# A causal convolution and a SwiGLU block on one core: the opening is put together anew

## The chip, the cores and the metric

The kernel runs on one core of one Trainium2 chip. Each core has a matrix engine (TensorE, PE in the profile, with its weight loads as PEld), a vector engine (VectorE, DVE), a scalar engine (ScalarE, ACT), a general engine (GpSimd, POOL) and a queue engine that issues transfers (SyncE, SP). Every engine works through its own instructions in the order in which the program gives them; they meet through semaphores. The metric is the time of one execution on the device in microseconds (us), the median of several runs.

## The reference

The input `x` has 8 sequences of 4096 tokens with 192 channels. Eight heads of 24 channels each have 7 taps, and the taps go through a softmax:

```python
w = np.exp(weight - np.max(weight, axis=-1, keepdims=True))
w = w / (np.sum(w, axis=-1, keepdims=True) + 1e-09)
x_pad = np.concatenate([np.zeros((B, pad, D)), x], axis=1)
out = np.einsum('hk,bskhg->bshg', w, x_unf)      # causal, 7 taps, per head
g = x @ w_gate                                   # x: the result above, 32768 x 192
silu = g * (1.0 / (1.0 + np.exp(-g)))
return silu * (x @ w_val) @ w_out                # 192 -> 1536 -> 192
```

All inputs and the output are float32. The kernel's products take fp16 operands and add up in float32.

## The kernel before

The 32768 tokens are cut into 32 pairs of 1024 tokens, each pair into two blocks of 512 (`TB`). A block goes through 12 chunks (`NCH`) of 128 hidden channels. In a chunk, `Block.first` makes gate and value products (L517 and L518) from the convolved block, `Block.gate` runs SiLU on ScalarE (L522) and the product with the value on VectorE (L524), and `Block.second` adds pieces of the output product (L529) of the block before, so that the second product of a block runs during the first product of the next. Blocks 0 and 1 together have chunks 0 to 23; "chunk 12" is the first chunk of block 1.

TensorE writes into eight banks of PSUM. In the steady part these are two banks for gates, three for values, one named `run` for the convolution's running sum, and two for the output sums. In block 0 the gates of the chunks listed in `PLAN["third"]` use the bank `run` as a third gate bank, which puts them in line with the convolution that uses it too.

The convolution of later pairs is done on the vector engines by three groups of channels and tokens: A (channels 0 to 127, first block), B (channels 128 to 191, both blocks) and C (channels 0 to 127, second block). Transfers (`emit_load`, issued at L103) bring x as 32 x 32 squares into `sqA` and `sqB`; a VectorE transpose (`emit_turn`, L114) makes `xtA` and `xtB`; then ScalarE starts a running sum and makes products (L444, L437), VectorE adds taps to it (L454, the last one writes `aD`), GpSimd makes the other products and adds everything up (L459, L466), and writes `xc` (L472). Two transfers (`swapped`, L420 and L421) make a copy `xs` with the halves of the partitions exchanged. `at_chunk` writes down behind which chunk each of these steps is issued; `PLAN["opening"]` gives these chunks for pair 1 (turn, start, ScalarE taps, VectorE taps, GpSimd taps, join, swap), and `PLAN["load"]` gives the chunks of the loads of later pairs, counted from the pair's own first chunk, chunk 8 at the earliest.

Pair 0 is made another way, on TensorE. The taps land in `taps`, go through the softmax (L232 to L240), and are repeated into `left`, in a high and a low fp16 part. The four `repeat` products (L306) spread them over token rows and `cut_band` (L314) cuts bands out of them, which gives the matrices `T`. `heads` and `halves` (products at L327) multiply windows of x by these bands. Block 0's x is cast into `x16`, block 1's into `x16p` (two casts on GpSimd, L227). For block 0 the sums go through `foldA`, `foldC` and `gather` (L370) to `D0`, `D1`, `D2`, the operands of the first 12 chunks. For block 1, `lateA(0)`, `lateA(1)` and `lateC` do this between the chunks of block 0, with two copies (`foldA1`, `foldC1`) and two exchanges by transfer (`swapA1`, `swapC1`, L632). The taps in a third form, `parts`, go through two small products (L391) and a sum (L397) to `wn`, the scalars that the vector engines' convolution uses from pair 1 on.

`warm` issues products of zeros on the bank `idle`. The program's order is the order of issue on every engine. A transfer waits in its queue for its data, and what stands behind it waits with it: `mark` (L414) puts an empty instruction into SP's queue that waits for the last piece of a first quarter of the output product, and the first piece of the next quarter on the same half of the array waits for that instruction. The first weights (chunks 0 to 3), the next (4 to 7), the last (8 to 11) and the output weights are loaded through GpSimd's queue (L162 and L569).

## Time and profile before

| | us |
|---|---|
| median of 3 runs | 778.95 (777.58 to 778.97) |
| the profiled execution | 780.57 |
| its span, first to last instruction | 778.8 |
| TensorE busy in the span | 766.3 (98%) |
| VectorE, ScalarE, GpSimd busy | 658.2, 659.0, 667.9 |
| granted TensorE clock, mean over the span | 0.996 |

The page divides the span into 40 slices of 19.5 us; a digit gives the busy tenths of a slice. A row of the list of groups reads: line, engine, operation, output and input by the program's names, shape, count, then busy time and the mean of one in ns, then the idle time ahead of it and what ended that. The chain of work follows the last instruction back to what released it, step by step. A busy TensorE isn't a TensorE at its peak: the granted clock and the distance between starts tell that.

The opening of the profiled execution has these times: first filler on TensorE 0.99, taps landed 3.41, first `repeat` product 6.39, first `heads` product 8.65, first gate product 12.15, chunk 0's second step 12.79, block 1's first product 27.43, first pieces of the output product 29.95.

### The profile page before, as it was taken

To read this page: it belongs to the slowest core of one execution; us is meant where nothing else is said; L and a number is where in the kernel's file an instruction comes from. 1 tells how busy PE (TensorE), PEld (TensorE's weight loads), DVE (VectorE), ACT (ScalarE), POOL (GpSimd) and SP (SyncE) were. 2 spreads that over 40 slices of the span, in tenths; PEclk is the share of its full clock that TensorE was granted. 3 is DMA by queue.
4 is the path that set the end of the run, shared out by engine and by line. 5 is a ranking of instruction groups with operands and counts; after the bars stand their busy time and mean duration, and the time that the engine had idled before them with its cause. 6 is when DMAs were issued, how large, how long until landed. Compare 5 with 4: busy or idle time off the path is not lost.

```text
span 778.8 us, 28276 instructions
## 1 busy us (share of the span) xinstructions
PE 766.3 (98%) x11033; PEld 531.3 (68%) x11033; DVE 658.2 (85%) x1041; ACT 659.0 (85%) x1189; POOL 667.9 (86%) x654
## 2 busy tenths in 40 slices
PE   7799999999999999999999999999999999999998
PEld 3576666666666666666766766666666666666666
DVE  5688888888888888888888888888888888888975
ACT  5688888888888888888888888888888888888875
POOL 6589988899888899888898888898888898888850
PEclk9899999999999999999999999999999999999999
DMA  9434443433443344443444443444443344343211
GB/s 151 87 78 88 84 97 83 87 89 83 87 99 82 80 94 84 89 97 81 83 87 90 87 92 83 84 84 96 84 92 88 80 85 95 83 94 87 64 46 53
DMA packets 255336, 67.27 MB, mean 86 GB/s; under 512 B 207975, under 2 KB 255201, under 8 KB 255201
## 3 DMA queue, kind: packets, MB, share of 16 engines
q1 hardware_dynamic: 252329, 63.69, 38.6%
q0 software_dynamic: 2800, 1.77, 1.7%
q8 instruction: 86, 1.41, 0.8%
q14 instruction: 49, 0.40, 0.2%
q10 hardware_dynamic: 72, 0.00, 0.0%
HBM read 29.64 MB, written 25.17 MB: 70 GB/s over the span
## 4 chain that ended last, share of the span: by engine, by line
PE 96%; DMA 1%; DVE 1%; POOL 1%; SPq 0%; issue 0%; ACT 0%; DVEq 0%; ACTq 0%
PE gate L517 57%; PE acc L529 32%; PE val L518 7%; DMA sqB<-in_x_dram 1%; DMA taps<-in_weight_dram 0%; POOL t L466 0%; SPq L103 0%; PE acc L724 0%; POOL t L459 0%; ACT L233 0%; PE val L724 0%; PE run L724 0%; PE acc L327 0%; DVE xtB L114 0%; DVE aD L454 0%
## 5 line engine op out<-in xcount | busy, mean ns | idle before, releaser
L524 DVE TENSOR_TENSOR h<-silu,val 128x512 f16<-128x512 f16 x768 | 509.4, 681 | 107.5 <-ACT silu L522 78.1
L522 ACT ACTIVATE silu<-gate 128x512 f16<-128x512 f32 x768 | 453.1, 594 | 99.4 <-PE val L518 82.7
L466 POOL TENSOR_TENSOR t<-t,t 128x512 f32<-128x512 f32 x310 | 393.4, 1269 | 59.7 <-ACT t L437 39.2
L518 PE MATMUL val<-xc,w_sb 64*128 64x512 f16 x1116 | 410.3, 377 | 0.0
L517 PE MATMUL gate<-xc,w_sb 64*128 64x512 f16 x1116 | 409.9, 376 | 0.0
L529 PEld LDWEIGHTS <-h 64*128 64x128 f16 x6048 | 292.5, 94 | 125.9 <-SPq L414 2.8
L529 PE MATMUL acc<-wo_sb,h 64*128 64x192 f16 x6048 | 364.7, 243 | 2.4 <-SPq L414 2.3
L518 PE MATMUL val<-xs,w_sb 64*128 64x512 f16 x1116 | 360.4, 377 | 0.0
L517 PE MATMUL gate<-xs,w_sb 64*128 64x512 f16 x1116 | 360.2, 376 | 0.0
L517 PEld LDWEIGHTS <-w_sb 64*128 64x128 f16 x2340 | 213.0, 94 | 104.5 <-issue 2.6
L518 PEld LDWEIGHTS <-w_sb 64*128 64x128 f16 x2340 | 210.9, 95 | 3.5 <-issue 3.3
L472 POOL TENSOR_TENSOR xc<-t,aD 128x512 f16<-128x512 f32 x93 | 118.0, 1269 | 7.3
L459 POOL TENSOR_SCALAR t<-xtA,wn 128x512 f32<-128x512 f32 x155 | 105.6, 691 | 9.2 <-DVE xtA L114 9.2
L437 ACT ACTIVATE t<-xtA,wn 128x512 f32<-128x512 f32 x124 | 88.5, 714 | 0.0
L567 ACT COPY o<-acc 128x384 f32<-128x384 f32 x126 | 60.3, 479 | 6.3 <-PE acc L529 3.4
L459 POOL TENSOR_SCALAR t<-xtB,wn 128x512 f32<-128x512 f32 x62 | 42.2, 694 | 4.5 <-DVE xtB L114 4.5
L454 DVE SCALAR_TENSOR_TENSOR aD<-xtA,wn,run 128x512 f32<-128x512 f32 x62 | 46.0, 742 | 0.0
L437 ACT ACTIVATE t<-xtB,wn 128x512 f32<-128x512 f32 x62 | 44.2, 713 | 0.0
L444 ACT ACTIVATE run<-xtA,wn 128x512 f32<-128x512 f32 x62 | 42.5, 686 | 0.0
L114 DVE STREAM_TRANSPOSE xtA<-sqA 128x544 f32<-128x544 f32 (+1 forms) x48 | 34.6, 721 | 0.0
L454 DVE SCALAR_TENSOR_TENSOR run<-xtB,wn,run 128x512 f32<-128x512 f32 x31 | 23.2, 750 | 0.2 <-ACT run L444 0.2
L454 DVE SCALAR_TENSOR_TENSOR run<-xtA,wn,run 128x512 f32<-128x512 f32 x31 | 23.2, 750 | 0.0
(105 smaller groups left out, 185.8 us busy)
## 6 DMA issues: line engine op xcount, KB each, us to landing
out_dram<-o SPq DMA_DIRECT2D x127, 192.0 KB, 2.0
sqA<-in_x_dram SPq DMA_DIRECT2D x92, 132.0 KB, 3.1
xs<-xc SPq DMA_DIRECT2D x186, 64.0 KB, 2.0
sqB<-in_x_dram SPq DMA_DIRECT2D x96, 68.0 KB, 2.3
headA<-in_x_dram SPq DMA_DIRECT2D x28, 128.0 KB, 2.6
headB<-in_x_dram SPq DMA_DIRECT2D x14, 68.0 KB, 2.2
headB<-in_x_dram SPq DMA_DIRECT2D x14, 64.0 KB, 2.0
w_sb<-in_moe_w_gate_dram POOLq DMA_DIRECT2D x3, 192.0 KB, 5.8
```

What stands on the lines that cost most here:

```text
L437: mul(parts[-1], *self.tap(k))
L444: nc.scalar.mul(self.aD, *self.tap(0))
L454: nc.vector.scalar_tensor_tensor(out=self.aD, in0=v, scalar=s, in1=run, op0=ALU.mult, op1=ALU.add)
L459: self.product(k, lambda t, v, s: nc.gpsimd.tensor_scalar(t, v, scalar1=s, scalar2=1.0, op0=ALU.mult, op1=ALU.mult), self.parts)
L466: nc.gpsimd.tensor_tensor(self.parts[0], self.parts[0], t, op=ALU.add)
L472: nc.gpsimd.tensor_tensor(xc, self.parts[0], self.aD, op=ALU.add)
L517: nc.tensor.matmul(g, w[0:DB, ca, f], a[0:DB, :], start=(i == 0), stop=(i == 2))
L518: nc.tensor.matmul(v, w[DB:P, cb, f], b[DB:P, :], start=(i == 0), stop=(i == 2))
L522: nc.scalar.activation(s, self.g.pop(j), AF.Silu)
L524: nc.vector.tensor_tensor(h, s, self.v.pop(j), op=ALU.mult)
L529: ins = nc.tensor.matmul(acc, self.h[j][r, ts(s, P)], wo_r[r, j, :], start=first and j == 0, stop=not first and j == NCH - 1, skip_group_c ...
L567: nc.scalar.copy(self.o[:, 2 * half : 2 * half + 2, :], self.acc[:, :, 0:D])
```

## The change

Taps: the transfer brings 8 rows of 7 instead of 64 rows with each head repeated eight times. A product with a mask `whose` (a new iota and two VectorE operations) writes the 64 rows into the bank `D2`; the maximum and the exponential read them there. `soft` gets an eighth column that holds 1e-9, and the sum over it is made on VectorE, in place of ScalarE's accumulation and an addition on GpSimd. The masks are made from integers by a helper `where`; the mask `band` is now made behind the maximum. A first exponential of a constant is issued behind the taps' transfer.

Order: three fillers stand ahead of the product with `whose` and three behind it, the one behind the repeats is gone, and short ones stand between the heads and a full one behind the gathers. The first weights for values are loaded right behind those for gates. ScalarE casts the first half of block 0's windows and GpSimd the second. `own` is copied on GpSimd. Block 1's x (`load_x(1, 0, NW)`) and the squares for group B are issued on SP behind the first `repeat` product; before, the x went out at the start and the squares behind the first heads. `parts` and the clearing of `x16p`'s other half are made on VectorE behind D1's copy, and the two small products for `wn` stand behind all the gathers.

Chunks: `lateA(0)` moves from 3 to 2, the second half of pair 1's A squares from behind `lateC` (8) to 9, group A's turn from 9 to 10, group B's swap from 14 to 12, the gates in the `run` bank from 2, 6, 9 to 2, 7, 10. The loads of pair 2 move from 8, 8, 14 and 20 to 10, 16, 18 and 21.

```diff
     opening=(
-        (9, 12, (13, 14), (13, 14), 12, 14, 20),
-        (2, 3, (4, 5), (3, 4), 4, 5, 14),
+        (10, 12, (13, 14), (13, 14), 12, 14, 20),
+        (2, 3, (4, 5), (3, 4), 4, 5, 12),
...
-    gate=2, val=3, lead=4, third=(2, 6, 9),
+    gate=2, val=3, lead=4, third=(2, 7, 10),
...
-    taps = const_pool.tile([RT, K], fp32, tag="taps", name="taps")
-    nc.scalar.dma_start(
-        out=taps[:, :],
-        in_=weight.unsqueeze(1).to_broadcast([H, 8, K]),
-    )
+    taps = const_pool.tile([H, K], fp32, tag="taps", name="taps")
+    nc.scalar.dma_start(out=taps, in_=weight)
...
-    load_x(1, 0, NW)
...
+    two = const_pool.tile([P, 1], fp32, tag="two", name="two")
+    nc.scalar.activation(two, one, AF.Exp)
...
+    head = numbers("head", [H, RT], [[1, RT]], 0, int32, -8)
...
+    def where(out, t, bits):
+        if bits:
+            nc.vector.tensor_scalar(t, t, scalar1=bits, scalar2=None, op0=ALU.bitwise_and)
+        nc.vector.tensor_scalar(out, t, scalar1=0.0, scalar2=None, op0=ALU.is_equal)
+
+    where(whose, head, -8)
+    where(rotate, far, 7)
+    where(pick[:, :, :].rearrange("r h m -> r (h m)"), row, 0)
...
     load_w(0, 4, 0)
+    load_w(0, 4, 1)
...
-    nc.vector.tensor_reduce(wmax, taps, axis=AX.X, op=ALU.max, negate=True)
-    nc.scalar.activation(soft, taps, AF.Exp, bias=wmax, accum_out=wsum)
-    nc.gpsimd.tensor_scalar(wsum, wsum, scalar1=1e-9, scalar2=None, op0=ALU.add)
+    warm(3)
+    rows = early["D2"][0:RT, 0:K]
+    nc.tensor.matmul(rows, whose, taps, start=True, stop=True)
+    nc.vector.tensor_reduce(wmax, rows, axis=AX.X, op=ALU.max, negate=True)
+    nc.scalar.activation(soft[:, 0:K], rows, AF.Exp, bias=wmax)
+    where(band, off, -8)
     nc.vector.memset(parity(x16p[:, 0, :, :], 1), 0.0)
...
+    nc.vector.tensor_reduce(wsum, soft, axis=AX.X, op=ALU.add)
...
-    cast(nc.gpsimd.tensor_copy, 0, 3)
-    load_w(0, 4, 1)
-    cast(nc.scalar.copy, 3, NW)
+    cast(nc.scalar.copy, 0, 3)
+    nc.scalar.activation(two, one, AF.Silu)
+    cast(nc.gpsimd.tensor_copy, 3, NW)
...
-    nc.scalar.copy(
+    nc.gpsimd.tensor_copy(
         own[:, :].rearrange("h (t c) -> h t c", t=2),
...
-    warm(6)
-    repeat(0, 0)
+    warm(3)
+    repeated_first = repeat(0, 0)
+
+    sync_after(nc.sync.nop(), repeated_first, "the rest after block 0's x")
+    load_x(1, 0, NW)
+    if n_pairs > 1:
+        for part in (2, 3):
+            emit_load(1, part, None)
     repeat(1, 0)
     repeat(0, HH)
     repeat(1, HH)
-    warm(1)
...
-    some = heads(0, 0)
-
-    if n_pairs > 1:
-        sync_after(nc.sync.nop(), some, "squares after x")
-        for part in (2, 3):
-            emit_load(1, part, None)
+    heads(0, 0)
+    warm(1, 2)
     heads(0, 1)
+    warm(1, 2)
     nc.scalar.copy(foldA, sums[0])
     heads(1, 0)
+    warm(1, 2)
     heads(1, 1)
...
+    gather("D1", 2, foldC, first=False)
+    gather("D2", 3, foldC)
+    warm(1)
+    nc.vector.tensor_copy(D1, early["D1"])
+    nc.scalar.copy(D2, early["D2"])
+    nc.vector.memset(parity(x16p[:, 1, :, :], 0), 0.0)
+
+    parts = const_pool.tile([RT, 3, K], fp16, tag="parts", name="parts")
+    raw, rest = (const_pool.tile([RT, K], fp32, tag=n, name=n) for n in ("raw", "rest"))
+    nc.vector.tensor_tensor(raw, soft[:, 0:K], norm.to_broadcast([RT, K]), op=ALU.mult)
+    nc.vector.tensor_copy(parts[:, 0, :], raw)
+    nc.vector.tensor_tensor(rest, raw, parts[:, 0, :], op=ALU.subtract)
+    nc.vector.tensor_copy(parts[:, 1, :], rest)
+    nc.vector.tensor_tensor(parts[:, 2, :], rest, parts[:, 1, :], op=ALU.subtract)
...
-    gather("D1", 2, foldC, first=False)
-    gather("D2", 3, foldC)
-    nc.vector.tensor_copy(D1, early["D1"])
-    nc.scalar.copy(D2, early["D2"])
...
-        if n_pairs > 1:
-            for part in (0, 1):
-                emit_load(1, part, 1)
...
-    at_chunk(3, lambda: lateA(0))
+    at_chunk(2, lambda: lateA(0))
     at_chunk(5, lambda: lateA(1))
     at_chunk(5, outA)
     at_chunk(8, lateC)
+    if n_pairs > 1:
+        for part in (0, 1):
+            at_chunk(9, lambda part=part: emit_load(1, part, 1))
...
-            at_chunk(max(base + c, 8), lambda q=q, part=part: emit_load(q, part))
+            c = {2: 10, 3: 16, 0: 18, 1: 21}[part] if q == 2 else base + c
+            at_chunk(c, lambda q=q, part=part: emit_load(q, part))
```

More of the change, by code (lines that the diff above doesn't have):

```diff
@@ L167, with numbers @@
     nc.vector.memset(one, 1.0)
+    two = const_pool.tile([P, 1], fp32, tag="two", name="two")
+    nc.scalar.activation(two, one, AF.Exp)
     nc.vector.memset(x_sb[0:pad, 0, 0, :], 0.0)
-    def numbers(name, shape, pattern, base, dt=fp32):
+    def numbers(name, shape, pattern, base, dt=int32, step=1):
         t = const_pool.tile(shape, dt, tag=name, name=name)
         nc.gpsimd.iota(
-            t, pattern=pattern, base=base, channel_multiplier=1, allow_small_or_imprecise_dtypes=True
+            t, pattern=pattern, base=base, channel_multiplier=step, allow_small_or_imprecise_dtypes=True
         )
         return t
-    far = numbers("far", [RT, 8, K], [[-1, 8], [1, K]], 8, int32)
+    head = numbers("head", [H, RT], [[1, RT]], 0, int32, -8)
+    far = numbers("far", [RT, 8, K], [[-1, 8], [1, K]], 8)
     row = numbers("row", [RT, RT], [[-1, RT]], 0)
-    off = numbers("off", [P, W], [[-1, W]], -(K // 2))
-    nc.vector.tensor_scalar(far, far, scalar1=7, scalar2=None, op0=ALU.bitwise_and)
+    off = numbers("off", [P, W], [[-1, W]], 0)
+    whose = const_pool.tile([H, RT], fp32, tag="whose", name="whose")
     rotate = const_pool.tile([RT, 8, K], fp32, tag="rotate", name="rotate")
-    nc.vector.tensor_scalar(rotate, far, scalar1=0.0, scalar2=None, op0=ALU.is_equal)
     pick = const_pool.tile([RT, H, 8], fp16, tag="pick", name="pick")
-    nc.vector.tensor_scalar(
-        pick[:, :, :].rearrange("r h m -> r (h m)"), row, scalar1=0.0, scalar2=None, op0=ALU.is_equal
-    )
-    nc.vector.tensor_tensor(off, off, off, op=ALU.mult)
     band = const_pool.tile([P, W], fp16, tag="band", name="band")
-    nc.vector.tensor_scalar(band, off, scalar1=float((K // 2) ** 2), scalar2=None, op0=ALU.is_le)
+    def where(out, t, bits):
[5 more added lines that the diff above has]
+    where(pick[:, :, :].rearrange("r h m -> r (h m)"), row, 0)
     plain = const_pool.tile([P, 4, grp], fp16, tag="plain", name="plain")
@@ L202 @@
     plain = plain[:, :, :].rearrange("p h c -> p (h c)")
+    nc.gpsimd.memset(spread, 0.0)
     load_w(0, 4, 0)
-    nc.gpsimd.memset(spread, 0.0)
+    load_w(0, 4, 1)
     mask = const_pool.tile([RT, D], fp16, tag="mask", name="mask")
-    nc.gpsimd.memset(mask, 0.0)
-    nc.gpsimd.affine_select(
-        out=mask[:, :].rearrange("r (h c) -> r h c", h=H),
-        in_=mask[:, :].rearrange("r (h c) -> r h c", h=H),
-        pattern=[[-8, H], [0, grp]],
-        compare_op=ALU.not_equal, fill=1.0, base=0, channel_multiplier=1,
-    )
     x16 = xpool.tile([P, NW, D + 8], fp16, tag="x16", name="x16", bufs=1)
@@ L230, with warm @@
     wmax, wsum, norm = (const_pool.tile([RT, 1], fp32, tag=n, name=n) for n in ("wmax", "wsum", "norm"))
-    soft = const_pool.tile([RT, K], fp32, tag="soft", name="soft")
-    nc.vector.tensor_reduce(wmax, taps, axis=AX.X, op=ALU.max, negate=True)
-    nc.scalar.activation(soft, taps, AF.Exp, bias=wmax, accum_out=wsum)
-    nc.gpsimd.tensor_scalar(wsum, wsum, scalar1=1e-9, scalar2=None, op0=ALU.add)
+    soft = const_pool.tile([RT, K + 1], fp32, tag="soft", name="soft")
+    nc.vector.memset(soft[:, K : K + 1], 1e-9)
+    opening = ctx.enter_context(ExitStack())
+    pool0 = opening.enter_context(tc.tile_pool(name="early", bufs=1, space=bass.MemoryType.PSUM))
+    early = {
+        n: pool0.tile([P, TB], fp32, tag=n, name=n)
+        for n in ("hiA", "loA", "hiC", "loC", "idle", "D2", "D0", "D1")
+    }
+    def warm(n, r=SUBS):
+        for _ in range(n):
+            nc.tensor.matmul(
+                early["idle"][:, 0 : r * P].rearrange("p (r c) -> p r c", c=P), zeros,
+                zeros.unsqueeze(1).to_broadcast([P, r, P]), start=True, stop=True,
+            )
+    warm(3)
[4 more added lines that the diff above has]
+    where(band, off, -8)
     nc.vector.memset(parity(x16p[:, 0, :, :], 1), 0.0)
     spun = const_pool.tile([RT, 8, K], fp32, tag="spun", name="spun")
-    nc.vector.tensor_tensor(spun, rotate, soft.unsqueeze(1).to_broadcast([RT, 8, K]), op=ALU.mult)
+    nc.vector.tensor_tensor(spun, rotate, soft[:, 0:K].unsqueeze(1).to_broadcast([RT, 8, K]), op=ALU.mult)
     turned = const_pool.tile([RT, 8], fp32, tag="turned", name="turned")
+    nc.vector.tensor_reduce(wsum, soft, axis=AX.X, op=ALU.add)
     nc.vector.tensor_reduce(turned, spun, axis=AX.X, op=ALU.add)
@@ L254 @@
     left = left[:, :, :, :].rearrange("r i n m -> r i (n m)")
-    two = const_pool.tile([P, 1], fp32, tag="two", name="two")
+    cast(nc.scalar.copy, 0, 3)
     nc.scalar.activation(two, one, AF.Silu)
-    cast(nc.gpsimd.tensor_copy, 0, 3)
-    load_w(0, 4, 1)
-    cast(nc.scalar.copy, 3, NW)
-    own = const_pool.tile([RT, P], fp16, tag="own", name="own")
-    nc.scalar.copy(
-        own[:, :].rearrange("h (t c) -> h t c", t=2),
-        mask[:, P:D].unsqueeze(1).to_broadcast([RT, 2, DB]),
-    )
-    nc.scalar.copy(
-        parity(x16p[:, 1, :, :], 0),
-        zeros[:, 0:grp].unsqueeze(1).unsqueeze(1).to_broadcast([P, NW, 4, grp]),
-    )
+    cast(nc.gpsimd.tensor_copy, 3, NW)
     for k, lo, hi, at in ((0, 0, DB, 0), (1, DB, 96, 0), (2, 0, 32, 32), (3, 32, 96, 0)):
@@ L272 @@
         )
-    parts = const_pool.tile([RT, 3, K], fp16, tag="parts", name="parts")
-    raw, rest = (const_pool.tile([RT, K], fp32, tag=n, name=n) for n in ("raw", "rest"))
-    nc.gpsimd.tensor_tensor(raw, soft, norm.to_broadcast([RT, K]), op=ALU.mult)
-    nc.gpsimd.tensor_copy(parts[:, 0, :], raw)
-    nc.gpsimd.tensor_tensor(rest, raw, parts[:, 0, :], op=ALU.subtract)
-    nc.gpsimd.tensor_copy(parts[:, 1, :], rest)
-    nc.gpsimd.tensor_tensor(parts[:, 2, :], rest, parts[:, 1, :], op=ALU.subtract)
     load_w(4, 8, 0)
     load_w(4, 8, 1)
-    opening = ctx.enter_context(ExitStack())
-    pool0 = opening.enter_context(tc.tile_pool(name="early", bufs=1, space=bass.MemoryType.PSUM))
-    early = {
-        n: pool0.tile([P, TB], fp32, tag=n, name=n)
-        for n in ("hiA", "loA", "hiC", "loC", "idle", "D2", "D0", "D1")
-    }
-    def warm(n, r=SUBS):
-        for _ in range(n):
-            nc.tensor.matmul(
-                early["idle"][:, 0 : r * P].rearrange("p (r c) -> p r c", c=P), zeros,
-                zeros.unsqueeze(1).to_broadcast([P, r, P]), start=True, stop=True,
-            )
+    nc.gpsimd.memset(mask, 0.0)
+    nc.gpsimd.affine_select(
+        out=mask[:, :].rearrange("r (h c) -> r h c", h=H),
+        in_=mask[:, :].rearrange("r (h c) -> r h c", h=H),
+        pattern=[[-8, H], [0, grp]],
+        compare_op=ALU.not_equal, fill=1.0, base=0, channel_multiplier=1,
+    )
+    own = const_pool.tile([RT, P], fp16, tag="own", name="own")
+    nc.gpsimd.tensor_copy(
+        own[:, :].rearrange("h (t c) -> h t c", t=2),
+        mask[:, P:D].unsqueeze(1).to_broadcast([RT, 2, DB]),
+    )
     T = const_pool.tile([P, 2, H, W], fp16, tag="T", name="T")
@@ L388 @@
     nc.scalar.copy(D0, early["D0"])
+    gather("D1", 2, foldC, first=False)
[11 more added lines that the diff above has]
+    nc.vector.tensor_tensor(parts[:, 2, :], rest, parts[:, 1, :], op=ALU.subtract)
+    wn = const_pool.tile([P, 2, K], fp32, tag="wn", name="wn")
     taps_ps = early["idle"][:, 0 : 6 * K].rearrange("p (g t k) -> p g t k", g=2, k=K)
@@ L391 @@
         nc.tensor.matmul(taps_ps[:, g, :, :], which, parts, start=True, stop=True)
-    gather("D1", 2, foldC, first=False)
-    gather("D2", 3, foldC)
-    nc.vector.tensor_copy(D1, early["D1"])
-    nc.scalar.copy(D2, early["D2"])
-    wn = const_pool.tile([P, 2, K], fp32, tag="wn", name="wn")
     nc.vector.tensor_reduce(wn, taps_ps.rearrange("p g t k -> p g k t"), axis=AX.X, op=ALU.add)
```

## The prediction

> **What bounds the kernel now.** I read the page first, then TensorE's waits over the first 80 us, then the clock in short stretches, then the chain of work and the transfer queue of the opening.

> ```profile
> span 778.8 us, 28276 instructions
> PE   7799999999999999999999999999999999999998
> PEclk9899999999999999999999999999999999999999
> PE 96%; DMA 1%; DVE 1%; POOL 1%; SPq 0%; issue 0%; ACT 0%; DVEq 0%; ACTq 0%
> ```

> TensorE is full from about 40 us to the end, so a microsecond won in the first two slices is a microsecond off the span, and nothing later can be won. The change touches only those slices. What TensorE waits for there (total us, times, longest):

> ```profile
> PE hiA L306 <- DVE left L249: 2.6, 1, 2.6
> PE gate L517 <- DVE aD L454: 2.5, 1, 2.5
> PE acc L529 <- SPq L414: 2.3, 1, 2.3
> PE val L518 <- DVE h L524: 0.6, 2, 0.3
> ```

> Three holes: before the first product, at gate chunk 6, and in block 1 before the third quarter of the second product. The next rows show a second price of the last two. Columns: stretch, its length, busy of PE, PEld, DVE, ACT, POOL (instructions), granted clock, DMA share, GB/s.

> ```profile
> 14.95:18.40 3.45, 3.19 (x113) 1.69 (x112) 2.38 (x5) 1.20 (x3) 0.12 (x1) 1.00 1.41 180
> 18.40:21.80 3.40, 0.93 (x28) 0.57 (x14) 2.94 (x5) 3.26 (x6) 3.24 (x4) 1.00 1.14 147
> 21.90:22.10 0.20, 0.20 (x4) 0.10 (x2) 0.00 (x0) 0.20 (x1) 0.20 (x1) 0.50 0.27 34
> 32.00:35.20 3.20, 0.87 (x19) 0.59 (x16) 1.92 (x4) 0.88 (x2) 2.79 (x3) 1.00 0.63 112
> 38.60:38.80 0.20, 0.20 (x6) 0.14 (x4) 0.20 (x1) 0.00 (x0) 0.00 (x0) 0.50 0.30 82
> ```

> After each hole the clock stands at 0.50, from 21.8 to 25.2 and from 35.45 to 38.85. Gate products then start 0.43 us apart instead of 0.215, and the first stretch costs 1.2 us on 2.44 us of gates plus 0.4 on the late sums (0.97 against 0.57), so 1.6 us; the second costs half of 3.4, so 1.7. [...]

> Where the second hole comes from (start, length, step of the chain):

> ```profile
> 10.76 6.64 DMA sqB<-in_x_dram
> 17.43 0.76 DVE xtB L114
> 18.26 0.70 ACT run L444
> 20.25 0.75 DVE aD L454
> ```

> Squares for the B channels land at 17.40, VectorE having waited 1.07 us, and gate 6 shares the `run` bank with that convolution. Where the third comes from, in the transfer queue:

> ```profile
> 25.80 1.10 SPq L632 DMA_DIRECT2D swapC<-foldC  x2
> 26.95 2.18 SPq L103 DMA_DIRECT2D sqA<-in_x_dram  x4
> 29.17 2.99 SPq L103 DMA_DIRECT2D sqB<-in_x_dram  x4
> 32.25 0.47 SPq L420 DMA_DIRECT2D xs<-xc  x1
> 32.76 0.59 SPq L421 DMA_DIRECT2D xs<-xc  x1
> 33.40 1.23 SPq L103 DMA_DIRECT2D sqA<-in_x_dram  x2
> ```

> SP issues without a pause from 25.80 to 34.63; the two marks (L414) stand behind that, and TensorE waits for them from about 32.4.

> **The change, part by part.** Times are in the profiled execution.

> *Taps to first product* (6.39 before). Taps land at 3.41 now. Eight rows in place of 64: bounds 2.4 (0.74 plus 1.7, the page's quickest small landing) and 3.41; no row is nearer to either, I take 2.9. The spreading product: a 21-column one takes 0.20, a 352-column one 0.52; I take 0.45 with the hand-over, so 3.35. `wmax` 0.15: 3.55. The table load of 1.28 us at 3.48 leaves the path: the dummy exponential does it from 1.25 or 1.95 (after ACT's issue of 1.21), done by 2.7 to 3.45, under the landing. Exp (0.30) lies beside what VectorE now does behind `wmax`: two mask operations (0.22, 0.20) and a clearing (0.30), till 4.27. Then spun 0.24, the new sum 0.19 (as `turned`, 0.20), and from `turned` to the end of `left` 0.89 as before (5.44 to 6.33): 5.6, TensorE at r = 5.67. With the bounds of the landing r is 5.2 to 6.15. The removed read of the accumulator (0.19) and GpSimd's sum (0.24) were in line and are gone. `whose`, the fourth iota and the other masks (0.1 to 0.24 each) end before 2.3, hidden behind the landing.

> *First product to chunk 0.* Before, the gates run as if unbroken from 12.58 (12.79 less one step of 0.215), r + 6.19. After: the fourth repeat is out at r + 1.58, and the heads start there, without the 0.53 of warm(1). Four heads of 0.42 (48 products: 0.84) and three short fillers of 0.21 end, with latency, at r + 4.07; before it was r + 4.17, so the filler eats the gain. foldC (0.42 then 0.37, in turn) and the last gathers as before: D1's copy runs from r + 5.47 to 6.15. Now the new wait: the taps product stands ahead of chunk 0 in TensorE's queue and needs `parts`, which moved from GpSimd (over at 9.0) to VectorE behind D1's copy: clearing 0.30, five small operations at 0.13 to 0.21 (I take 0.15), hand-over and product 0.15. Chunk 0 at r + 7.35 = 13.02: 0.44 later than before, bounds 12.3 to 13.6. Everything in chunk 0 waits behind it, and SiLU and VectorE wait for that.

> *x and weights.* The second x block goes out behind the first product, about 6.2, not 2.3; it took 6.6, so 12.8; GpSimd's two casts (1.28) end at 14.1, before the late sums want them at 14.95 (chunk 2, moved from 3). Those casts now hold the last weights in GpSimd's queue: issued 14.1 and 14.75 against 11.44 and 12.07, landing in 5.8 and 6.1, at 20.9; chunk 8 wants them at 21.1. Cost zero, with a slack of 0.2 (bounds: 1.0 of stall, if r is early and a landing takes 6.8, and none). The output weights (8.8) arrive by 25.3, wanted after 26.6. The other moved issue, the value weights of chunks 0 to 3, goes 6.17 to 3.3 and cannot hurt: wanted at 12.2. Swapped casts (0.66 each) end by 5.5, `own` by 8.6, both before their readers.

> *Squares B.* Four issues behind x, until about 8.7 instead of 11.37; even with 6.64 they land at 15.4. VectorE turns them after chunk 2's product: 16.36 moves to c0 + 3.78 = 16.80, so the landing is hidden and the turn moves from 17.43 to 16.80. From there to `aD` 3.57 as before: 20.37. TensorE needs `aD` at chunk 7, not 6: it does chunk 6 meanwhile, at 18.85, when SiLU 4 (behind `run` on ScalarE) is over. Its idle is 0.70 + 0.92 = 1.6 of a 3.4 us stretch against 2.47. I take it that the clock holds, by nearness to neither row (busy 53%; 27% dropped, 92% held), because the idle is split and VectorE hides part of it.

> *To chunk 12.* Chunk 7 at 20.42, then VectorE's pace: chunk 8 done 21.7, late sum C 22.3, ScalarE through SiLU 8 at 23.0, foldC1 at 23.4. The exchange took 2.41 from foldC1 to its use (25.78 to 28.19), so chunk 12 ends at 25.9 (24.5 to 24.95 of work, then a wait of 0.8) against 28.3: 2.4 won.

> *Marks.* SP now: exchange C 23.45 to 24.55, four sqA (2.18) to 26.8, two sqB (1.2 to 1.5) to 28.3, swap B at chunk 12 (1.1) to 29.4; its data is ready, GpSimd's `xc` taking 7.6 from the turn, 24.4. The other six loads stand behind the marks, at chunks 16, 18 and 21. TensorE arrives, by ScalarE's pace of before (28.28 to SiLU 14's end and chunk 16), at 29.95, against 34.83: 2.48 more won, slack 0.5. Then the clock stretch of 1.7 is gone. The loads for pair 2 are wanted at chunks 22 and 30, landing in 3.1 us, hidden; without that cover one costs 3 us.

> *Sum.* 2.4 + 2.48 + 1.7 = 6.6. Against this execution's own 780.57 (span 778.8 and 1.8 around it) that is 774.0; the median of the runs is 778.95, 1.62 lower, so 772.4.

> **The rivals.**
> - *The clock halves once more*, after the remaining 1.6 us of idle or the 1.4 us before chunk 0. For: 27% busy did it twice. Against: half is far from that. Price 1.6 (the measured stretch): 774.0.
> - *Both half-clock stretches stay, whatever the holes do*, each beginning at its place for a cause that the trace doesn't name: 1.6 + 1.7 on top, 775.7. Against: each begins 0.6 to 0.8 us after a hole's end, and none stands where there is no hole. [...]
> - *The marks stay late*: SP's slack of 0.5 goes if the sqB issues take longer (one took 1.38). Full price 2.5 + 1.7: 776.6. Against: six issues fewer.
> - *Squares are no earlier*, the x block's 432 KB standing before them on the same queue: the first gain goes, 774.8. Against: they would have to take 8 us from their issue. With the marks late as well: 779.0, no change.
> - *Slower: the x block lands so late that GpSimd's casts hold the late sums and the last weights.* With landing L, TensorE waits L - 13.55 at chunk 2 and 0.45 more at chunk 8, so the loss is L - 13.1. It outweighs 6.6 and the 1.6 of noise from L = 21.3, fifteen us after its issue; the slowest landing on the page is 8.8. At L = 22 it gives 781.

> **How the numbers follow.** Forecast 0.55 at 772.4 (its own range 771.2 to 773.5, from r and the small operations); clock once 0.15, both stretches 0.03; marks 0.11; squares 0.05; those two together 0.04; slower 0.07, which also stands for queue effects that I can't see. A time within 0.2% (1.6 us) is what a measurement can't tell from no change. Faster 0.89, same 0.04, slower 0.07. The range takes in all cases up to the marks, and below the forecast the earliest landing of taps with a clock that is up by the heads (0.6 on fillers and gathers more): 770.6 to 776.8.

> **What would show it.** No table load behind the taps; chunk 0 near 13; xtB turned right behind the third h, with no wait for a transfer; gate 7, not 6, behind `aD`, with under 1 us in one piece; no wait on L414's successor; granted clock 1.00 from 14 to 60. I am wrong if TensorE still waits over 2 us in one piece after 14, if the clock shows 0.50 behind 20, or if a wait for weights or x stands at chunks 2 or 8.

## The result, and the profile after

The changed kernel takes 775.59 us (median of 6 runs, 774.35 to 776.25). The kernel before, run beside it, takes 778.96 (777.58 to 779.67). The ratio is 0.9956, 95% interval 0.9943 to 0.9969: 3.4 us won, where the forecast was 6.55. The profiled executions differ by more, 780.57 against 775.71, so by 4.9.

The page of the kernel after, the lines that answer to those of before:

```profile
span 773.9 us, 28289 instructions
PE   8999999999999999999999999999999999999998
PEclk9999999999999999999999999999999999999999
PE 98%; DVE 1%; DMA 0%; issue 0%; ACT 0%; SPq 0%; DVEq 0%; ACTq 0%
```

TensorE's second slice has gone from 7 to 9, and POOL has left the chain that ends last. What TensorE waits for over the first 80 us of after (total us, times, longest):

```profile
PE idle L404 <- DVE parts L400: 1.2, 1, 1.2
PE idle L239 <- DVE one L162: 1.0, 1, 1.0
PE gate L525 <- DVE aD L462: 0.7, 1, 0.7
PE acc L537 <- SPq L422: 0.2, 1, 0.2
PE hiA L301 <- DVE left L265: 0.2, 1, 0.2
```

The three holes of before (2.6, 2.5 and 2.3 us) are down to 0.2, 0.7 and 0.2. A new one of 1.2 us stands ahead of chunk 0: `idle` L404 is the product that spreads `parts`. (The row of 1.0, the first dummy products waiting for their ones at the very start, stands in before too and is no loss.) The chain of work shows what the new hole does (start, length, step):

```profile
10.55 0.69 DVE D L390
11.25 0.30 DVE x16p L392
11.60 0.32 DVE parts L397
12.54 0.17 PE idle L404
12.75 0.43 PE gate L525
13.18 0.41 PE val L526
17.14 0.21 PE gate L525
20.34 0.75 DVE aD L462
```

A clearing and five operations run on VectorE in line behind D1's copy while TensorE stands still. After that the products of chunks 0 to 2 come 0.43 us apart, until 15.5; from then on they come 0.21 apart. So TensorE was at half speed for the first 2.9 us of chunk work. It had been so before the hole too: the first products of zeros, from 1.0 us on, are 0.41 apart, and equal products of 512 columns just ahead of the hole 0.40. In one trace the changes of the granted clock on record lie whole multiples of 3.41 us apart (11.55, 21.79, 25.21, 35.45 and 38.86 in before); the expectations below call a step of 3.41 us a window.

The transfer queue (SP) of after, around the marks:

```profile
23.63 1.10 SPq L640 DMA_DIRECT2D swapC<-foldC  x2
24.78 3.28 SPq L103 DMA_DIRECT2D sqA<-in_x_dram  x4
28.10 1.03 SPq L103 DMA_DIRECT2D sqB<-in_x_dram  x2
29.23 0.47 SPq L428 DMA_DIRECT2D xs<-xc  x1
29.74 0.59 SPq L429 DMA_DIRECT2D xs<-xc  x1
30.55 0.97 SPq L103 DMA_DIRECT2D sqB<-in_x_dram  x2
32.24 0.42 SPq L567 DMA_DIRECT2D out_dram<-o  x1
32.71 2.51 SPq L103 DMA_DIRECT2D sqA<-in_x_dram  x2
```

Where SP issued without a pause from 25.80 to 34.63 before, it is now through at 30.33 with what stands ahead of the marks (L422 here), since six loads stand behind them, and TensorE waits 0.2 us for them.

Where the time is won and lost is read best by when a gate chunk's first product starts (us from the span's start, of one profiled execution each; the other kernels are described below, `before_again` is a second execution of before):

| gate chunk | before | before_again | before_loads_new | loads_old | after | parts_early | parts_early_no_fillers |
|---|---|---|---|---|---|---|---|
| 0 | 12.15 | 12.13 | 12.63 | 12.60 | 12.60 | 11.78 | 10.10 |
| 3 | 14.51 | 15.00 | 14.78 | 17.23 | 16.75 | 14.44 | 12.71 |
| 7 | 21.69 | 21.02 | 21.27 | 21.48 | 21.13 | 19.12 | 17.48 |
| 13 | 28.20 | 25.91 | 26.16 | 26.36 | 26.03 | 24.01 | 24.03 |
| 17 | 36.18 | 33.99 | 32.00 | 34.00 | 31.53 | 29.95 | 28.76 |
| 19 | 39.30 | 35.80 | 33.81 | 37.43 | 33.34 | 31.76 | 30.57 |
| 40 | 60.63 | 57.13 | 55.81 | 59.25 | 55.60 | 53.63 | 52.58 |

In after the first product comes 2.05 us earlier than before (4.34 against 6.39), chunk 0 is 0.45 later, and chunk 3 is 2.2 later. Of these 2.2, some 0.66 are the products of `lateA(0)`, which stand ahead of chunk 3 now and stood behind it before. After is ahead by 2.2 at chunk 13, by 6.0 at chunk 19 and by 5.0 at chunk 40.

### The profile page after: what moved, and what is told of

It reads as the page before. It is cut to its first block, busy times and chain, and to the rows that moved or that the text cites. A ratio compares the mean times of both kernels' runs of the same rounds, so it can differ in the third digit from the quotient of the medians.

```text
span 773.9 us, 28289 instructions
## 1 busy us (share of the span) xinstructions
PE 767.2 (99%) x11038; PEld 658.8 (85%) x11038; DVE 659.6 (85%) x1051; ACT 662.8 (86%) x1187; POOL 668.5 (86%) x650
## 3 DMA queue, kind: packets, MB, share of 16 engines
q8 instruction: 86, 1.41, 0.8%
## 4 chain that ended last, share of the span: by engine, by line
PE 98%; DVE 1%; DMA 0%; issue 0%; ACT 0%; SPq 0%; DVEq 0%; ACTq 0%
PE val L526 41%; PE acc L537 30%; PE gate L525 25%; DMA xs<-xc 0%; PE acc L733 0%; PE acc L322 0%; PE D L370 0%; PE hiC L322 0%; PE hiA L322 0%; PE val L733 0%; PE run L733 0%; PE idle L239 0%; DVE h L532 0%; DVE aD L462 0%; DVE D L390 0%
## 5 line engine op out<-in xcount | busy, mean ns | idle before, releaser
L537 PE MATMUL acc<-wo_sb,h 64*128 64x192 f16 x6048 | 432.7, 243 | 0.3 <-SPq L422 0.2
L537 PEld LDWEIGHTS <-h 64*128 64x128 f16 x6048 | 388.6, 94 | 41.3 <-SPq L422 1.4
L114 DVE STREAM_TRANSPOSE xtA<-sqA 128x544 f32<-128x544 f32 (+1 forms) x48 | 34.6, 721 | 0.0
```

The source lines that it names most:

```text
L537: ins = nc.tensor.matmul(acc, self.h[j][r, ts(s, P)], wo_r[r, j, :], start=first and j == 0, stop=not first and j == NCH - 1, skip_group_c ...
```

## The experiments

The theory after the result: the rewritten front wins two microseconds up to the first product and gives them back through the hole behind D1's copy and the half clock; what is left of the gain is the transfers' new chunks. Its rivals: the fillers eat the front's gain; the earlier squares or the new third banks carry the measured gain; or the front does carry it, as the 2.2 us at chunk 13 suggest.

**parts_early: the hole taken away.** After, with the clearing and the five operations moved ahead of the heads, behind the last band product:

```diff
+    nc.vector.memset(parity(x16p[:, 1, :, :], 0), 0.0)
+    parts = ...
+    nc.vector.tensor_tensor(raw, soft[:, 0:K], norm.to_broadcast([RT, K]), op=ALU.mult)
...
     nc.vector.tensor_copy(D1, early["D1"])
     nc.scalar.copy(D2, early["D2"])
-    nc.vector.memset(parity(x16p[:, 1, :, :], 0), 0.0)
-    parts = ...
...
```

> Edit: in the changed kernel the clearing and the five small operations that make parts stand on VectorE behind the bands (where VectorE is idle from 6.7 to 9.05), not behind D1's copy. Theory 1 (the 1.2 us hole ahead of chunk 0 holds the clock down and costs itself): the wait of 1.18 on parts is gone, chunk 0 starts near 11.4 instead of 12.6, and gate products come 0.215 apart well before 15.5; 1.2 plus 1 to 1.5 us won, 773.0 to 773.4 against 775.6. Theory 2 (the clock comes up late in any case, since what runs before chunk 0 is too thin): chunk 0 starts 1.2 earlier and its products stay 0.43 apart until about 15.5; at most 1.2 won, 774.4 or more.

Measured: 773.64 us (773.49 to 775.07), ratio 0.9941 [0.9922, 0.9960], 2.0 below after; the spans differ by 2.0 as well (771.9 against 773.9). The wait on `parts` is gone, VectorE does that work from 7.38 to 8.67, and the gate products are 0.215 apart from 12.0 on. Chunk 0 comes 0.8 earlier and chunk 3 2.3 earlier, and nearly all of that (1.97) is still there at chunk 40. So the hole and the slow products behind it cost after some 2 us. The slow products are not the hole's doing alone: third_old, below, has such a hole too (1.1 us), and behind it products 0.215 apart.

**no_fillers: the three short fillers taken out.**

```diff
     heads(0, 0)
-    warm(1, 2)
     heads(0, 1)
-    warm(1, 2)
...
-    warm(1, 2)
     heads(1, 1)
```

> Edit: the changed kernel without the three short fillers between the heads. They took 0.33 us each on TensorE, in line with the heads. Theory 1 (they only lengthen the path while the clock is down): heads end 1.0 earlier, chunk 0 near 11.6, 1.0 won, 774.6. Theory 2 (they carry the clock): the clock comes up later than 15.5 or not before the next window's end, and the time is the same or worse, 775.6 to 777.

Measured: 775.03 us (774.34 to 775.16), ratio 0.9950 [0.9931, 0.9969]: not told apart from after. From the first head to the last it takes 1.35 us less, 0.45 for each filler. The heads begin 0.64 later in this execution, though (the second `left` took 0.68 where after has 0.25), so the last filler ahead of the hole comes 0.94 earlier, and the hole grows by nearly as much. TensorE's longest wait in this kernel:

```profile
PE idle L401 <- DVE parts L397: 2.1, 1, 2.1
```

VectorE's timeline and GpSimd's there (start, length, instruction) show why the small operations did not move up as far:

```profile
10.84 0.59 DVE L394 CAST parts<-raw 64x7 f16<-64x7 f32 x1
11.66 0.32 DVE L396 CAST parts<-rest 64x7 f16<-64x7 f32 x1
10.13 1.27 POOL L222 CAST x16p<-x_sb 94x576 f16<-94x576 f32 x2 [1.83 <-DMA x_sb<-in_x_dram]
```

A cast of 64x7 took 0.59 beside GpSimd's casts and 0.17 without (in parts_early_no_fillers). Here the first products behind the hole are 0.215 apart, and the clock is at half from 12.95 to 16.37. So fillers alone are not the cause; the next run suggests that they cost their time once the hole is gone.

**parts_early_no_fillers: both.** The two edits above together.

> Both edits: parts behind the bands and no short fillers. If the two losses add, chunk 0 starts near 10.4 and the time is 772 to 773; if the squares (issued until 8.7, landing in some 6 us) become the next wait, VectorE's turn of the B squares waits for a transfer and only part of it is won, 773.5. If the fillers carry the clock, it is no better than parts behind the bands alone.

Measured: 772.72 us (772.43 to 773.07), ratio 0.9925 [0.9908, 0.9943]: 2.9 below after, and 0.9 below parts_early, whose interval overlaps. Chunk 0 is at 10.10, 2.5 us earlier than in after. Of that, a part is taken by a new wait at chunk 12:

```profile
PE gate L523 <- DMA swapA<-foldA: 1.4, 1, 1.4
```

The exchange of group A (swapA) landed in 5.8 us (median), where it took 2.0 in after. The output weights, 576 KB issued at 12.38, took 10.6 us, so both were under way together.

**before_again: the kernel before once more, unchanged, one execution.**

> The kernel before once more, for a second profile: is the first one (780.57, 1.6 above the median of the runs) typical? Theory 1: holes at gate 6 and at the marks are there again, each with a half-clock stretch of 3.4 us behind it, within 0.3 us of the first profile. Theory 2: the clock's windows fall another way in this execution, one of the stretches is missing or shorter, and the time is 777.5 to 779.5.

Measured: 777.10 us, span 775.3, 3.5 less than the execution that the prediction was worked from. Its waits of TensorE are the same three, of other sizes:

```profile
PE acc L529 <- SPq L414: 2.8, 1, 2.8
PE hiA L306 <- DVE left L249: 2.5, 1, 2.5
PE gate L517 <- DVE aD L454: 1.3, 1, 1.3
```

and the clock (columns: stretch, length, busy of PE, PEld, DVE, ACT, POOL with instructions, granted clock, DMA share, GB/s) falls in another place:

```profile
7.20:10.60 3.40, 3.40 (x102) 1.94 (x99) 1.87 (x5) 1.22 (x3) 3.11 (x10) 0.50 0.70 94
34.20:37.20 3.00, 3.00 (x66) 2.78 (x62) 1.73 (x3) 2.22 (x4) 0.00 (x0) 1.00 0.32 82
```

It is at half from about 7.2 to 14.0, behind the hole before the first product, and at full behind the marks' hole of 2.8 us, where it had been at half in the first execution. Chunk 13 comes at 25.91, 2.3 earlier than in the first execution and 0.1 earlier than in after. So the 2.2 us that after seems to be ahead at chunk 13 belong to one execution of before, not to the kernel; before_loads_new, below, with the old front, has 26.16 there.

**loads_old: after, with the transfers' chunks of before.**

```diff
-        (2, 3, (4, 5), (3, 4), 4, 5, 12),
+        (2, 3, (4, 5), (3, 4), 4, 5, 14),
...
-            at_chunk(9, lambda part=part: emit_load(1, part, 1))
+            at_chunk(8, lambda part=part: emit_load(1, part, 1))
...
-            c = {2: 10, 3: 16, 0: 18, 1: 21}[part] if q == 2 else base + c
-            at_chunk(c, lambda q=q, part=part: emit_load(q, part))
+            at_chunk(max(base + c, 8), lambda q=q, part=part: emit_load(q, part))
```

> Edit: in the changed kernel the chunks of the transfers are put back (group B's exchange at 14, the second half of pair 1's A squares at 8, the loads of pair 2 at 8, 8, 14 and 20). Theory 1 (the marks stood late behind SP's issues, and moving these is what freed them): TensorE waits 2.3 to 3 us for the marks again instead of 0.2, and the time is 2.2 to 4.5 us longer, 777.8 to 780.1, the upper end if the clock halves behind it. Theory 2 (the marks came free because the rest of the opening moved): within 0.5 us of 775.6.

Measured: 779.28 us (777.69 to 780.56, 10 runs), ratio 1.0003 [0.9992, 1.0014]. The whole gain is gone. The marks' wait is back, and the half clock behind it (waits first, then the clock of a stretch, columns as above):

```profile
PE acc L537 <- SPq L422: 2.3, 1, 2.3
```

```profile
34.20:37.20 3.00, 3.00 (x34) 2.25 (x31) 0.69 (x1) 1.48 (x3) 0.00 (x0) 0.50 0.31 81
```

The wait is 2.1 longer than in after and 3.4 us at half clock cost 1.7: 3.8 together, which is the difference of the two spans (777.6 against 773.9, 3.7).

**before_loads_new: before, with the new chunks alone.** The same lines the other way round.

> Edit: the kernel before with the new chunks of the transfers and nothing else. Theory 1 (late marks are a loss of their own): the wait for the marks falls from 2.3 to 2.8 us to under 0.5, and the time from 779.1 to 775.5 to 777, by whether the clock used to halve there. Theory 2 (another wait takes its place): 778 or more.

Measured: 775.69 us (774.47 to 775.78), ratio 0.9954 [0.9939, 0.9969]: as fast as the whole change. Its waits of TensorE:

```profile
PE hiA L306 <- DVE left L249: 2.7, 1, 2.7
PE gate L517 <- DVE aD L454: 1.8, 1, 1.8
PE acc L529 <- SPq L414: 1.0, 2, 0.5
```

The two holes of the old front are all there, and the time is that of after. These two runs settle it from both sides: the transfers' chunks carry the measured gain, and the front as it was changed carries none. All the chunks move together in both, so which of them carries it isn't separated.

**squares_old: after, with x at the start and the squares behind the first head.**

```diff
+    load_x(1, 0, NW)
...
-    sync_after(nc.sync.nop(), repeated_first, "the rest after block 0's x")
-    load_x(1, 0, NW)
...
-    heads(0, 0)
+    some = heads(0, 0)
+    if n_pairs > 1:
+        sync_after(nc.sync.nop(), some, "squares after x")
+        for part in (2, 3):
+            emit_load(1, part, None)
```

> Edit: in the changed kernel block 1's x goes out at the start again and the B squares behind the first heads. Theory 1 (what the prediction had: the move is what brings the squares early): they are issued from about 6.4 instead of 5.25, land late enough that VectorE waits for them, and 0.5 to 2.4 us are lost, 776.1 to 778. Theory 2 (they are early because the heads are 2.9 us earlier, wherever they are issued): VectorE's turn comes right behind the third product without a wait, and the time is within 0.5 us of 775.6.

Measured: 775.59 us (774.83 to 776.79), ratio 0.9959 [0.9943, 0.9974]: no change. The squares go out at 6.62, xtB is turned at 17.96 right behind the third h, and VectorE doesn't wait for them. They are in time because the heads come earlier now, not because of what they are issued behind.

**third_old: after, with the third gate banks of before.**

```diff
-    gate=2, val=3, lead=4, third=(2, 7, 10),
+    gate=2, val=3, lead=4, third=(2, 6, 9),
```

> Edit: in the changed kernel the gates in the bank run are those of chunks 2, 6 and 9 again. Theory 1 (the bank couples gate 6 to the convolution): TensorE waits 1.4 to 1.7 us in one piece at chunk 6 for aD and chunk 7 is 0.6 later; 0.6 us lost, or 2.2 if the clock halves behind it, 776.2 to 777.8. Theory 2 (VectorE's pace sets chunks 6 to 9 in any case): within 0.3 us of 775.6.

Measured: 776.86 us (775.74 to 777.59), ratio 0.9967 [0.9953, 0.9981]. The median is 1.3 above after's, but the intervals overlap. The wait for `aD` is 1.8 us in one piece where after has 0.7, and the clock holds; at chunk 16 the profile is only 0.1 behind after's. But this profile can't price the banks. It is of the fastest of six executions, and its products are fast from chunk 0 on, behind a hole of 1.1 us on `parts`: chunk 0 starts at 13.26 and chunk 3 at 15.87, where after has 12.60 and 16.75. The banks' worth is between nothing and 1.3 us; these runs don't say more.

Then four versions of parts_early_no_fillers, to see what stands in its way.

**x_at_start: the second x block and the squares issued as in squares_old.**

> Edit: on the kernel with parts behind the bands and no short fillers, block 1's x goes out at the start and the B squares behind the first heads, as before the change. That kernel waits 1.4 us at chunk 12 for swapA, whose transfer takes 5.8 us there (2.1 in the kernel before) while weights and squares are in flight. Theory 1 (the x block sent late pushes the casts, the last weights and the output weights behind it into the time of the exchange): GpSimd's casts run 2 to 3 us earlier, swapA lands in 2 to 4 us, the wait is gone and 1 to 1.4 us are won, 771.3 to 771.8. Theory 2 (the transfers are bound as a whole, whatever their order): the wait moves to the first x windows or stays, and the time is 772.4 to 773.2.

Measured: 772.06 us (771.81 to 772.81), ratio 0.9913 [0.9898, 0.9928]. swapA lands in about 3.2 us and the wait of 1.4 is gone. GpSimd's casts start at 8.44 and not 9.89, so the output weights go out at 10.93 and not 12.38, further from the exchange. The gain of 0.7 is not told apart from nothing by the intervals.

**swap_c_30: the exchange of group C in the third row of `opening` one chunk earlier, 30 for 31.**

> Edit: on the same kernel group C's exchange is issued behind chunk 30 in place of 31. TensorE loses 0.35 us at chunk 36, where it waits 0.2 for xs in the trace. Theory 1 (issued too late by half a microsecond): chunk 36 takes 0.98 again and 0.3 is won, 772.4, at the edge of what can be told. Theory 2 (xc of group C isn't ready by then, and SP holds the marks behind the wait): no change or a loss of up to 1 us.

Measured: 772.13 us (771.99 to 773.24), ratio 0.9917 [0.9901, 0.9934]. Chunk 36 loses its 0.35 us no more. In this execution swapA landed in about 4 us and the wait of 1.4 did not occur, so that wait differs from execution to execution.

**early_no_first_exp: without the first dummy exponential.**

```diff
-    nc.scalar.activation(two, one, AF.Exp)
```

> Edit: the same kernel without the first exponential. Theory 1 (with the hole gone, the start of the softmax is on the path): the table load of 1.28 us stands behind the taps again, the first product comes near 5.6 instead of 4.34, chunk 0 is 1.2 to 1.3 later, and 0.6 to 1.3 us are lost, 773.3 to 774.0. Theory 2 (what is won at the start is lost to the transfers at chunk 12 anyway): under 0.3 lost.

Measured: 772.22 us (771.81 to 773.59), ratio 0.9917 [0.9902, 0.9932]: nothing lost. ScalarE's timeline without the dummy, and then that of before:

```profile
1.36 1.28 ACT L247 ACT_TABLE_LOAD   x1 [1.36 <-PEq L763]
```

```profile
3.48 1.28 ACT L233 ACT_TABLE_LOAD   x1 [3.48 <-DMA taps<-in_weight_dram]
```

Without the dummy the table load starts at 1.36 all the same and is over 0.37 us before Exp, which starts when `wmax` is there. In before, whose Exp read the tile that the transfer wrote, the load stood behind the taps' landing; the new Exp reads what the spreading product left. So, as far as these traces show, it is the product that moves the load, and the dummy adds nothing.

**x_start_swap_30: x_at_start and swap_c_30 together.**

> Both edits, x at the start and group C's exchange behind chunk 30. If both gains are real and add, 771.0 to 771.5; if neither is, 772.4 to 773.5.

Measured: 771.91 us (771.11 to 772.86), ratio 0.9910 [0.9895, 0.9925]: the fastest of all, 0.9% below before and 3.7 us below after, though not told apart from either edit alone.

## Why the prediction was right and wrong

The sign and the range were right; the gain was half of the forecast. The miss of 3.2 us (775.6 against 772.4) is two pieces: 1.7 between the profiled executions (775.7 against 774.0) and 1.5 in the step from there to the median. The 1.7 are some 0.6 by which TensorE passed the marks later than in the sum, and 1.0 that was lost after chunk 19.

*From the profiled execution to the median.* This step failed. It subtracted 1.62, as if the execution after would stand as far above its median as the one before. After's stands 0.1 above. What had made before's execution slow were the two stretches at half clock, and the sum took both out in full and then took the 1.62 off as well. The second execution of before has neither, its clock falls elsewhere: chunk 13 comes 2.3 us earlier and chunk 19 3.5, which is the whole difference of the two spans (778.8 and 775.3). "To chunk 12: 2.4 won" measured 2.2 against the first execution and nothing against the second.

*Marks.* Right, and all of the measured gain. The wait went from 2.3 to 0.2, and the stretch of 1.7 with it; putting the old chunks back returned 3.7 us. TensorE passed the marks at 30.53 rather than 29.95, so 0.6 later than in the sum; up to chunk 12 it was 0.1 late. There was luck in the short wait: SP was done ahead of the marks at 30.33 and not at 29.4, which is more than the slack of 0.5, because four sqA issues took 3.28 and not 2.18. The wait stayed at 0.2 because TensorE was late as well.

*Taps to first product, 5.67 with bounds from 5.2.* It came at 4.34, below the lower bound. The taps had landed by 2.39, when the spreading product started, which is the landing of the lower bound; `whose` had been done at 2.02. Below that bound it came mainly by what follows: from `spun` to the end of the first `left` VectorE took 0.73, where the sum had 1.32. The first `left` took 0.25 where before had 0.58, and no GpSimd instruction ran beside it. The reason given for the table load was wrong too, as early_no_first_exp shows.

*First product to chunk 0, r + 7.35.* Measured r + 8.26. The fillers cost 0.45 each and not 0.21: the heads start 0.88 apart in after and 0.41 in before. D1's copy ended at r + 6.90 and not r + 6.15, of which the fillers are some 0.7; from there to chunk 0 it took 1.36 and not 1.20. The wait itself was seen and placed rightly. What was missing is a price behind it: the sum took the products of chunks 0 to 2 at full speed, as they ran in the first execution of before. From chunk 0's first gate product to chunk 2's last it took 3.27 us in after, 2.14 and 2.65 in the two executions of before, and 1.76 in parts_early. This is where the 2 us won at the first product went. The rival "the clock halves once more" (0.15) names this place, "the 1.4 us before chunk 0", and nearly this price, but not what happened: no product of 512 columns in after ran at full speed ahead of 15.5, so the clock came up late rather than fell once more. The sign "granted clock 1.00 from 14 to 60" was met by the record alone; up to 15.5 the distance between products says half.

*Squares B and the banks.* xtB was turned at 17.52 right behind the third h, without a wait for a transfer, and gate 7 waited 0.7 behind `aD`: as written. But "four issues behind x" was not the cause (squares_old), and the turn was 0.7 late for the reason just given. The clock held behind `aD`: the record of after has no change from 15.76 to 773.52.

*x and weights.* No wait for weights or x in after: right. The second x block landed 5.1 us after its issue.

*What was missed late.* The lead of after over before falls from 6.0 us at chunk 19 to 5.0 at chunk 40. Some 0.3 went at chunk 20, behind marks that stood in SP's queue after the two sqA issues at 32.71 that took 2.51, and 0.34 at chunk 36, where `xs` of group C came late; 0.2 at chunk 23 have no cause on record. The sum had priced the loads that were moved there at nothing.

*Still open.* What brings the clock up at the start. The first products of zeros are 0.41 apart in before and after, so TensorE begins at half speed there, and the clock record of both traces begins with the step up: at 11.55 in before and 15.76 in after. In the others the distance between equal products tells it. Gate products are 0.42 to 0.43 apart up to 12.63 in before_loads_new, 15.97 in loads_old and 16.05 in squares_old, and 0.21 to 0.23 apart from 13.05, 17.23 and 17.60 on; in the six kernels with `parts` made early they are 0.21 to 0.23 apart from between 10.1 and 12.4 on. In before_again the clock fell at 7.19 and rose again at 14.02. The hole on `parts` doesn't settle it: behind one of 1.2 us (after, loads_old) and of 1.1 (squares_old) the products began slow, behind one of 1.1 in third_old they were fast from the first at 13.26 on. In no_fillers they were fast from 12.28 on, and the clock fell at 12.95, behind the hole. Work without a break isn't enough: in after TensorE was busy from 5.53 to 8.94, on heads and fillers, and the products that followed, of 512 columns, were still 0.40 apart.

## What to carry to other kernels

When TensorE waits for a mark, a semaphore or a small transfer, look at what stands in the issuing queue ahead of it: here, moving a few loads by some chunks was worth all of this change (3.7 us between loads_old and after), and a rewritten front was worth nothing until its own new wait was taken away. Before a product is put at the head of the busy engine's queue, give its inputs a place where that engine has other work; six small operations moved up by 4 us were worth 2 us here. When one profiled execution has stretches at half clock, take a second execution of the same kernel before counting their end as a gain: a stretch that only one of them has is no sure gain, and it must not be taken off the sum and off the median both.

## What the runs showed of the hardware

*The views show a granted clock of 1.00 up to its first recorded change, and that can be wrong.* In after they say 1.00 throughout, while products of one kind were 0.43 us apart until 15.5 and 0.21 from then on; the first change on record is at 15.76. The distance between equal products is the surer reading.

*A small VectorE operation took longer beside a GpSimd instruction in these cases.* A 64x7 cast took 0.59 us beside GpSimd's casts (no_fillers, above) and 0.17 without them (parts_early_no_fillers). In parts_early the second `left` (64x96), started 0.02 us after a GpSimd cast, took 0.77; in parts_early_no_fillers it started 0.01 us ahead of the same cast and took 0.25, and the cast took 0.76 instead of 0.66. Why, the traces don't show.

*The same issues on SP took different times.* Four of the same sqA loads took 2.18 us in before and 3.28 in after, and two took 1.23 in before and 2.51 in after.
